# First row tile in chunks, second tile's gate values between the first one's up values, sigmoid table loaded later

## Chip, cores, metric

One core of a Trainium2 chip runs the kernel. The metric is the device time of one execution in microseconds; smaller is better. All runs told of here are at a granted clock of 0.999 or 1.0 in the records. Kernels are compared only within the same rounds. Times in the text are us. A time "at" which something happens counts from the start of the profiled span.

## The reference

```python
x = A_x                                   # 1 x 2048 x 640, bf16
xn = _layernorm(x, axis=-1)
s = _A_ref(xn, k_cache, v_cache, wq, wo)  # 32 heads of 192, the last 512 keys
g = _silu(_B_ref(xn, w_gate, w_up, w_down))
return x + s * g

def _B_ref(x, w_gate, w_up, w_down):      # 640 -> 1536 -> 640
    h = _sigmoid(x @ w_gate) * (x @ w_up)
    return h @ w_down
```

The kernel does the B part first, in four blocks of 512 rows. The first block is taken in four tiles of 128 rows, so that PE can begin as soon as 128 rows are normalised. The change touches nothing but these four tiles, and of those mostly the first two. The rest of the B part (until about 164 us in the trace) and the attention part behind it are the same in both kernels.

## The kernel before

```python
# loads: x of tile 0 on SP, x of tile 1 on ACT's queue, then the weights by pieces on SP
load_x(0, 1)
load_x(1, 1, nc.scalar)
load_f(nc.sync, wg_sb, wg_r, 0, 4, 0, 3)
load_f(nc.sync, wg_sb, wg_r, 0, 4, 3, NCD)
load_f(nc.sync, wu_sb, wu_r, 0, 4, 0, 3)      # "wu's first piece"
load_x(2, 1)
load_f(nc.sync, wu_sb, wu_r, 0, 4, 3, NCD)    # "wu's last chunks"
# ... cut ...

def stats_end(t):                             # rstd
    nc.vector.bn_aggr(mv[:], ln[t][:])
    if t == 0:
        nc.scalar.activation(rstd[:], mv[:, 1:2], AF.Sqrt, bias=eps_t[:], scale=1.0)
        nc.scalar.activation(junk[:], eps_t[:], AF.Sigmoid)   # loads the sigmoid table
        stats_half(1, 0)
        nc.vector.reciprocal(rstd[:], rstd[:])
    else:
        nc.vector.tensor_scalar(rstd[:], mv[:, 1:2], eps, None, op0=ALU.add)
        nc.gpsimd.tensor_tensor(rstd[:], rstd[:], mhalf[:], ALU.pow)

def turn_pe(t):          # 5 transposes on PE into PSUM, then two copies to xnT (3 + 2 chunks)
    engs = (nc.vector, nc.scalar) if t == 0 else (nc.scalar, nc.scalar)
    # ... cut ...

def tile_gates(t, amid): # 20 matmuls with wg, 20 with wu; turn_pe(t + 1) inside the wu ones
    for half, w in ((0, wg_sb), (1, wu_sb)):
        for c in range(NCD):
            if half == 1 and c == amid:
                turn_pe(t + 1)
            for f in range(FT):
                nc.tensor.matmul(bank[k][:, half, f * P:(f + 1) * P], ...)
    # sigmoid on ACT, product on VectorE: cut

dummy(18); dummy(6, 64)                       # idle matmuls that bring PE to full clock speed
# ... tile 0's statistics ...
normal(0, ((0, 3 * P), (3 * P, D)))
stats_half(1, 1)
turn_pe(0)
dummy(2)
# ... tiles 1 to 3 normalised ...
m0 = tile_gates(0, 3)                         # then tiles 1, 2, 3
# ... cut ...
for f in range(FT, NF):
    gated(0, f, k, norm_piece(1, f - FT))     # "the first gated block" begins here
```

The softmax here doesn't subtract the row's maximum and nothing guards it: scores larger than these inputs give would overflow.

Of the kernel before, what the change touches and what calls it, by code (L numbers as in the profile page):

```python
# [8 lines left out]
AF = mybir.ActivationFunctionType  # L9
ALU = mybir.AluOpType  # L10
BF16 = mybir.dt.bfloat16
# [4 lines left out]
def kernel(  # L16
# [13 lines left out]
    nc = tc.nc  # L30
    P = 128
    H2 = 64

    xf = A_x.flatten_outer_dims()
    of = out.flatten_outer_dims()
    S, D = xf.shape
# [8 lines left out]
    TB = 512  # L45
    NB = S // TB
    TQ = TB // P
    NT = S // P
    NCD = D // P
    NF = F // P  # L50
# [6 lines left out]
    eps = 1e-5  # L57
# [11 lines left out]
    bank = [psum.tile([P, 2, 512], F32, name=f"bank{i}") for i in range(4)]  # L69
# [4 lines left out]
    ident = const.tile([P, P], BF16, name="ident")  # L74
    mhalf = const.tile([P, 1], F32, name="mhalf")
    eps_t = const.tile([P, 1], F32, name="eps_t")
    junk = const.tile([P, 1], F32, name="junk")
    warm = const.tile([P, 256], BF16, name="warm")

    xnT = pers.tile([P, NB, NCD, TB], BF16, name="xnT")  # L80
# [5 lines left out]
    wg_r = B_w_gate.rearrange("(c p) f -> p c f", p=P)  # L86
# [56 lines left out]
    with ExitStack() as bctx:  # L143
        wB = bctx.enter_context(tc.tile_pool(name="wB", bufs=1))
        xpool = bctx.enter_context(tc.tile_pool(name="xpool", bufs=4))
        bwork = bctx.enter_context(tc.tile_pool(name="bwork", bufs=4))
        hpool = bctx.enter_context(tc.tile_pool(name="hpool", bufs=2))

        wg_sb = wB.tile([P, NCD, F], BF16, name="wg_sb")
        wu_sb = wB.tile([P, NCD, F], BF16, name="wu_sb")  # L150
# [1 line left out]

        xt = {}

        def load_x(t, n, eng=nc.sync):

            x = xpool.tile([P, n, D], BF16, name=f"x_sb{n}", bufs=4 if n == 1 else 2)
            if eng is nc.scalar:

                nc.vector.memset(x[:, 0, 0:2], 0.0)  # L160
            eng.dma_start(x[:], xf[t * P:(t + n) * P, :].rearrange("(q p) d -> p q d", p=P))  # L161
            for i in range(n):
                xt[t + i] = x[:, i, :]

        def load_f(eng, w, r, f0, f1, c0=0, c1=NCD):
            eng.dma_start(w[:, c0:c1, f0 * P:f1 * P], r[:, c0:c1, f0 * P:f1 * P])  # L166

        nc.vector.memset(warm[:], 0.0)
        load_x(0, 1)
        load_x(1, 1, nc.scalar)  # L170
        load_f(nc.sync, wg_sb, wg_r, 0, 4, 0, 3)
        load_f(nc.sync, wg_sb, wg_r, 0, 4, 3, NCD)
        load_f(nc.sync, wu_sb, wu_r, 0, 4, 0, 3)
        load_x(2, 1)
        load_f(nc.sync, wu_sb, wu_r, 0, 4, 3, NCD)
        load_x(3, 1)
# [3 lines left out]
        load_x(TQ, TQ)  # L180
        nc.sync.dma_start(wd_sb[:], wd_r)
        load_x(2 * TQ, TQ)
        nc.vector.memset(eps_t[:], eps)
        nc.scalar.activation(junk[:], eps_t[:], AF.Sqrt)
        nc.gpsimd.memset(mhalf[:], -0.5)
        make_identity(nc, ident[:])
# [2 lines left out]
        def dummy(n, cols=256):  # L189
            for _ in range(n):  # L190
                nc.tensor.matmul(bank[1][:, 1, 0:cols], lhsT=warm[:, 0:P], rhs=warm[:, 0:cols],
                                 start=True, stop=True)

        ln = {}

        def stats_half(t, i):
            if i == 0:
                ln[t] = bwork.tile([P, 2, nc.vector.BN_STATS_DIM], F32, name="st")
            nc.vector.bn_stats(ln[t][:, i, :], xt[t][:, i * (D // 2):(i + 1) * (D // 2)])

        def stats_end(t):
            mv = bwork.tile([P, nc.vector.BN_AGGR_DIM], F32, name="mv")
            rstd = bwork.tile([P, 1], F32, name="rstd")
            nc.vector.bn_aggr(mv[:], ln[t][:])
            if t == 0:
                nc.scalar.activation(rstd[:], mv[:, 1:2], AF.Sqrt, bias=eps_t[:], scale=1.0)
                nc.scalar.activation(junk[:], eps_t[:], AF.Sigmoid)
                stats_half(1, 0)
                nc.vector.reciprocal(rstd[:], rstd[:])
            else:  # L210
                nc.vector.tensor_scalar(rstd[:], mv[:, 1:2], eps, None, op0=ALU.add)
                nc.gpsimd.tensor_tensor(rstd[:], rstd[:], mhalf[:], ALU.pow)
            ln[t] = mv, rstd

        def normal(t, parts=((0, D),)):
            mv, rstd = ln[t]
            xn = xpool.tile([P, D], BF16, name="xn")
            for d0, d1 in parts:
                nc.vector.tensor_scalar(xn[:, d0:d1], xt[t][:, d0:d1], mv[:, 0:1], rstd[:, 0:1],
                                        op0=ALU.subtract, op1=ALU.mult)  # L220
            ln[t] = xn

        def turn_pe(t):

            engs = (nc.vector, nc.scalar) if t == 0 else (nc.scalar, nc.scalar)
            parts = []
            for i, (c0, c1) in enumerate(((0, 3), (3, NCD))):
                bk = bank[3][:, t % 2, :] if t or i == 0 else bank[2][:, 0, :]
                pT = bk[:, 0:NCD * H2].bitcast(BF16).rearrange("p (c n) -> p c n", c=NCD)
                for c in range(c0, c1):  # L230
                    nc.tensor.transpose(pT[:, c, :], ln[t][:, c * P:(c + 1) * P], ident[:])  # L231
                parts.append((engs[i], xnT[:, 0, c0:c1, t * P:(t + 1) * P], pT[:, c0:c1, :]))
            for eng, dst, src in parts:
                if eng is nc.vector:
                    nc.vector.tensor_copy(dst, src)
                else:
                    nc.scalar.activation(dst, src, AF.Copy)

        def turn_dma(t):
            q = t % TQ  # L240
# [2 lines left out]
        hT = {}  # L243
# [25 lines left out]
        def norm_piece(b, i):  # L269

            t = b * TQ + i

            def step():
                if i > 0:
                    normal(t - 1)
                    turn_dma(t - 1)
                if i < TQ:
                    stats_half(t, 0)
                    stats_half(t, 1)
                    stats_end(t)  # L280

            return step if i <= TQ else None


        FT = 4

        def tile_gates(t, amid):

            if 0 not in hT:
                hT[0] = hpool.tile([P, NF, TB], BF16, name="hT")  # L290
            k = t % 3
            r = slice(t * P, (t + 1) * P)



            for half, w in ((0, wg_sb), (1, wu_sb)):
                for c in range(NCD):
                    if half == 1 and c == amid:
                        turn_pe(t + 1)
                    for f in range(FT):  # L300
                        nc.tensor.matmul(bank[k][:, half, f * P:(f + 1) * P],  # L301
                                         lhsT=w[:, c, f * P:(f + 1) * P], rhs=xnT[:, 0, c, r],
                                         start=(c == 0 and f == 0), stop=(c == NCD - 1),
                                         skip_group_check=True)
            sig = bwork.tile([P, TB], BF16, name="sig")
            nc.scalar.activation(sig[:], bank[k][:, 0, :], AF.Sigmoid)
            return lambda: nc.vector.tensor_tensor(
                hT[0][:, 0:FT, r], bank[k][:, 1, :].rearrange("p (f n) -> p f n", f=FT),
                sig[:].rearrange("p (f n) -> p f n", f=FT), ALU.mult)

        dummy(18)
        dummy(6, 64)
        stats_half(0, 0)
        stats_half(0, 1)
        stats_end(0)
        normal(0, ((0, 3 * P), (3 * P, D)))
        stats_half(1, 1)
        turn_pe(0)
        dummy(2)
        stats_end(1)  # L320
        normal(1)
        stats_half(2, 0)
        stats_half(2, 1)
        stats_end(2)
# [1 line left out]
        stats_half(3, 1)  # L326
        normal(2)
        stats_end(3)
        m0 = tile_gates(0, 3)
        m0()  # L330
        normal(3)
        m1 = tile_gates(1, 1)
        m1()
        m2 = tile_gates(2, 1)
        m2()
        m3 = tile_gates(3, None)
        m3()
        k = 1
        for f in range(FT, NF):
            gated(0, f, k, norm_piece(1, f - FT))  # L340
            k = (k + 1) % 4
        for b in range(1, NB):
            for f in range(2):
                gated(b, f, k)
                k = (k + 1) % 4
            for q in range(TQ):
                down(b - 1, q, k)
                k = (k + 1) % 4
            if b == 1:
                load_x(3 * TQ, TQ)  # L350
            for f in range(2, NF):
                gated(b, f, k, norm_piece(b + 1, f - 4) if b + 1 < NB and f >= 4 else None)
                k = (k + 1) % 4
# [6 lines left out]
        for q in range(TQ):  # L360
            down(NB - 1, q, k)
            k = (k + 1) % 4
# [12 lines left out]
        for u in range(2):  # L375
            qT[u] = qpool.tile([P, 2 * DJ, TB], BF16, name="qT")
            for m in range(DJ):
                k = next(ks)
# [257 lines left out]
```

## Time and profile before

| | before |
|---|---|
| time, median of the runs (range) | 922.08 (921.9 to 922.63) |
| span of the profiled run | 920.8 |
| PE busy | 914.8, 99% |
| first matmul on wg | 6.20 |
| first gated block (L251) | 16.58 |
| from there to the end of the span | 904.2 |

### The profile page before, as it was taken

Reading aid. Unit: us, or ns where it says so; the run is one execution under the profiler, and the core shown is the slowest. Engines: PE = TensorE matmul, PEld = TensorE weight load, DVE = VectorE, ACT = ScalarE, POOL = GpSimd, SP = SyncE. Lnnn points to the kernel's source line nnn. Section 1 sums busy time; section 2 is a strip of 40 time slices with the busy share of each in tenths; the row PEclk is TensorE's granted clock in tenths of the full one; section 3 lists DMA queues with packets and bytes.
Section 4 is the critical chain, followed back from the end, with each engine's and each line's share of the span. In section 5 each row is a group of like instructions: output and inputs, shape, how many; then the busy total and the mean of one; then the engine's idle time right before and its main releaser. Section 6 shows DMA issues by size and latency. Waiting matters only on the chain.

```text
span 920.8 us, 25187 instructions
## 1 busy us (share of the span) xinstructions
PE 914.8 (99%) x11444; PEld 629.1 (68%) x11462; DVE 491.2 (53%) x982; ACT 302.3 (33%) x333; POOL 133.5 (15%) x158
## 2 busy tenths in 40 slices
PE   9999999999999999999999999999999999999998
PEld 7445455466868686767676777777776767686875
DVE  5452522445646464645555555545564646464677
ACT  4222222254142424233333333242414151515150
POOL 1000100001002000200120011001100111075633
PEclk9999999999999999999999999999999999999999
DMA  9320340115344434342426162616251615263535
GB/s 322 79 30 1 89 86 1 43 62 87 75 67 105 87 56 84 93 99 42 98 79 113 36 104 79 113 28 113 65 105 46 117 61 90 67 120 104 90 79 137
DMA packets 163147, 77.14 MB, mean 84 GB/s; under 512 B 140992, under 2 KB 158608, under 8 KB 163040
## 3 DMA queue, kind: packets, MB, share of 16 engines
q1 hardware_dynamic: 155936, 53.85, 29.9%
q0 software_dynamic: 5808, 20.52, 7.9%
q8 instruction: 89, 1.46, 0.7%
q10 hardware_dynamic: 1296, 1.16, 0.4%
q14 instruction: 18, 0.15, 0.1%
HBM read 39.45 MB, written 2.62 MB: 46 GB/s over the span
## 4 chain that ended last, share of the span: by engine, by line
PE 98%; DMA 1%; DVE 0%; SPq 0%; issue 0%; DVEq 0%
PE bank L494 22%; PE bank L423 21%; PE bank L445 19%; PE bank L405 18%; PE bank L251 10%; PE bank L263 6%; PE bank L371 1%; PE bank L301 1%; DMA wu_sb<-in_B_w_up_dram 1%; PE bank L529 0%; DVE o_sb L475 0%; DVE gate L480 0%; SPq L166 0%; SPq L161 0%; PE bank L231 0%
## 5 line engine op out<-in xcount | busy, mean ns | idle before, releaser
L409 ACT ACTIVATE E<-bank 128x1024 bf16<-128x1024 f32 x256 | 255.3, 1022 | 456.7 <-PE bank L405 456.6
L423 PE MATMUL bank<-xnT,wq_sb 64*128 64x512 bf16 x1800 | 226.4, 376 | 0.0
L494 PE MATMUL bank<-wo_sb,oT 64*128 64x320 bf16 x2688 | 205.2, 296 | 0.0
L405 PE MATMUL bank<-qT,kT 64*128 64x512 bf16 x1536 | 200.7, 376 | 0.0
L445 PE MATMUL bank<-vbuf,E 64*128 64x193 bf16 x4096 | 195.5, 243 | 0.0
L445 PEld LDWEIGHTS <-E 64*128 64x128 bf16 x4096 | 178.8, 94 | 10.4 <-issue 0.5
L494 PEld LDWEIGHTS <-oT 64*128 64x128 bf16 (+1 forms) x2892 | 163.3, 94 | 30.8 <-issue 0.5
L430 DVE CAST qT<-bank 128x1024 bf16<-128x1024 f32 x90 | 110.2, 1224 | 128.5 <-PE bank L423 128.5
L423 PEld LDWEIGHTS <-wq_sb 64*128 64x128 bf16 x1800 | 106.0, 100 | 87.1 <-issue 0.4
L405 PEld LDWEIGHTS <-kT 64*128 64x128 bf16 x1536 | 88.1, 94 | 73.5
L458 DVE TENSOR_TENSOR o_st<-bank,rden 128x768 bf16<-128x768 f32 x128 | 122.5, 957 | 4.8 <-DMA out_dram<-gate 0.4
L509 DVE TENSOR_TENSOR acc<-bank,acc 128x640 f32<-128x640 f32 x96 | 79.0, 823 | 20.3 <-PE bank L494 20.3
L118 POOL DMA_DIRECT2D vbuf<-in_A_v_cache_dram x28 | 21.1, 753 | 312.7 <-PE bank L445 309.8
L428 DVE COPY seen<-bank 128x2 f32<-128x2 f32 x90 | 14.3, 159 | 79.1 <-PE bank L423 79.1
L457 DVE RECIPROCAL rden<-bank 128x4 f32<-128x4 f32 x128 | 23.3, 182 | 60.6 <-PE bank L445 59.8
L251 PE MATMUL bank<-xnT,wg_sb 128*128 128x512 bf16 x216 | 54.5, 379 | 0.2
L251 PE MATMUL bank<-xnT,wu_sb 128*128 128x512 bf16 x215 | 54.4, 379 | 0.3
L257 DVE TENSOR_TENSOR hT<-bank,sig 128x512 bf16<-128x512 f32 x44 | 30.3, 689 | 42.7 <-ACT sig L254 42.7
L263 PE MATMUL bank<-wd_sb,hT 128*128 128x128 bf16 (+1 forms) x376 | 52.4, 297 | 0.4
L254 ACT ACTIVATE sig<-bank 128x512 bf16<-128x512 f32 x44 | 26.3, 597 | 68.4 <-PE bank L251 65.3
L263 PEld LDWEIGHTS <-hT 128*128 128x128 bf16 x384 | 29.7, 98 | 23.1
L251 PEld LDWEIGHTS <-wu_sb 128*128 128x128 bf16 x220 | 21.5, 98 | 26.0
(56 smaller groups left out, 366.6 us busy)
## 6 DMA issues: line engine op xcount, KB each, us to landing
wo_sb<-in_A_wo_dram SPq DMA_DIRECT2D x7, 960.0 KB, 5.5
wq_sb<-in_A_wq_dram POOLq DMA_DIRECT2D x7, 960.0 KB, 6.0
k_st<-in_A_k_cache_dram POOLq DMA_DIRECT2D x14, 384.0 KB, 5.4
vbuf<-in_A_v_cache_dram POOLq DMA_DIRECT2D x28, 192.0 KB, 3.6
row<-in_A_x_dram POOLq DMA_DIRECT2D x16, 160.0 KB, 2.8
oT<-o_st SPq DMA_TRANSPOSE x128, 3.4
x_sb<-in_A_x_dram SPq DMA_DIRECT2D x3, 640.0 KB, 9.9
wd_sb<-in_B_w_down_dram SPq DMA_DIRECT2D x1, 1920.0 KB, 13.5
```

Of the source, the lines that this page charges most:

```text
L251: nc.tensor.matmul(bank[k][:, half, 0:r1 - r0], lhsT=w[:, c, f * P:(f + 1) * P], rhs=xnT[:, b, c, r0:r1], start=(c == 0), stop=(c == NCD - 1))
L254: nc.scalar.activation(sig[:, 0:r1 - r0], bank[k][:, 0, 0:r1 - r0], AF.Sigmoid)
L257: nc.vector.tensor_tensor(hT[b][:, f, r0:r1], bank[k][:, 1, 0:r1 - r0], sig[:, 0:r1 - r0], ALU.mult)
L263: nc.tensor.matmul(wide(k)[:, d0:d1], lhsT=hT[b][:, f, q * P:(q + 1) * P], rhs=wd_sb[:, f, d0:d1], start=(f == 0), stop=(f == NF - 1))
L405: nc.tensor.matmul(bank[k][:, i, :], lhsT=kT[r, pr, j, c * P:(c + 1) * P], rhs=q[r, pr * DJ + j, :], start=(j == 0), stop=(j == DJ - 1))
L409: nc.scalar.activation(E[u, pr][:, c, :, :], bank[k][:], AF.Exp, scale=scale_qk)
L423: nc.tensor.matmul(bank[k][:, half, :], lhsT=wq[r, c, col:col + DJ * (P - 1) + 1:DJ], rhs=xnT[r, b, c, :], start=(c == 0 and not second), ...
L430: nc.vector.tensor_copy(qT[u][:, 2 * m:2 * m + 2, :], bank[k][:])
L445: nc.tensor.matmul(o4[:, q, 0:DH + 1], lhsT=e[r, c, h % 2, q * P:(q + 1) * P], rhs=vbuf[r, h, c, 0:DH + 1], start=(turn == 0 and qq == 0 a ...
L458: nc.vector.tensor_tensor(o_st[u][:, :, h * DH:(h + 1) * DH], o4[:, :, 0:DH], rden[:].to_broadcast([P, TQ, DH]), ALU.mult)
L494: nc.tensor.matmul(res[:, half, :], lhsT=oT[u][r, cc, q * P:(q + 1) * P], rhs=wo[r, cc, half * HD:(half + 1) * HD], start=(turn == 0 and c ...
L509: nc.vector.tensor_tensor(cols(acc[:, t, :]), res, cols(acc[:, t, :]), ALU.add)
```

## The change

Its intent is to give PE real work sooner. Tile 0 is normalised, turned and copied in pieces of one, two and two chunks of 128 columns, and each piece is multiplied when it is there, where before five chunks were turned together. Since all copies of tile 0 now go through ACT, the sigmoid table (1.28 of ACT time) is loaded only after the copies of tile 1. Tile 1's rstd uses ACT's square root, whose table is still loaded. Tile 1's 20 matmuls with wg go between tile 0's first and last matmuls with wu, so that wu's last chunks have longer to arrive. Wg's first piece moves to ACT's queue, tile 1's x to SP's.

```diff
-        load_x(1, 1, nc.scalar)
-        load_f(nc.sync, wg_sb, wg_r, 0, 4, 0, 3)
+        load_x(1, 1)
+        load_f(nc.scalar, wg_sb, wg_r, 0, 4, 0, 3)
 ... cut ...
-            if t == 0:
+            if t < 2:
                 nc.scalar.activation(rstd[:], mv[:, 1:2], AF.Sqrt, bias=eps_t[:], scale=1.0)
-                nc.scalar.activation(junk[:], eps_t[:], AF.Sigmoid)
-                stats_half(1, 0)
+                if t == 0:
+                    stats_half(1, 0)
                 nc.vector.reciprocal(rstd[:], rstd[:])
 ... cut: turn_pe(t, c0, c1, k) turns and copies a range of chunks, all copies on ACT;
     tile_gates becomes tile_half(t, half, c0, c1), tile_sigmoid(t), tile_gated(t) ...
-        normal(0, ((0, 3 * P), (3 * P, D)))
+        normal(0, ((0, P), (P, 3 * P), (3 * P, D)))
+
+        turn_pe(0, 0, 1)
+        turn_pe(0, 1, 3, 2)
+        tile_half(0, 0, 0, 1)
+        turn_pe(0, 3, NCD, 1)
+        tile_half(0, 0, 1)
         stats_half(1, 1)
-        turn_pe(0)
-        dummy(2)
         stats_end(1)
-        normal(1)
+        normal(1, ((0, 3 * P), (3 * P, D)))
+
+        tile_half(0, 1, 0, 2)
+        turn_pe(1, 0, 3)
+        tile_half(0, 1, 2, 3)
+        turn_pe(1, 3, NCD, 2)
+        nc.scalar.activation(junk[:], eps_t[:], AF.Sigmoid)
+        tile_half(1, 0)
+        tile_half(0, 1, 3)
+        tile_sigmoid(0)
 ... cut: tiles 2 and 3 as before, with turn_pe(t + 1) after the first chunk of wu ...
```

More of the change, by code (lines that the diff above doesn't have):

```diff
@@ L153, with load_x @@
         xt = {}
-        def load_x(t, n, eng=nc.sync):
+        def load_x(t, n):
             x = xpool.tile([P, n, D], BF16, name=f"x_sb{n}", bufs=4 if n == 1 else 2)
-            if eng is nc.scalar:
-                nc.vector.memset(x[:, 0, 0:2], 0.0)
-            eng.dma_start(x[:], xf[t * P:(t + n) * P, :].rearrange("(q p) d -> p q d", p=P))
+            nc.sync.dma_start(x[:], xf[t * P:(t + n) * P, :].rearrange("(q p) d -> p q d", p=P))
             for i in range(n):
@@ L168 @@
         nc.vector.memset(warm[:], 0.0)
+        nc.vector.memset(eps_t[:], eps)
+        nc.vector.memset(wg_sb[:, 0, 0:2 * P], 0.0)
         load_x(0, 1)
-        load_x(1, 1, nc.scalar)
-        load_f(nc.sync, wg_sb, wg_r, 0, 4, 0, 3)
+        load_x(1, 1)
+        load_f(nc.scalar, wg_sb, wg_r, 0, 4, 0, 3)
         load_f(nc.sync, wg_sb, wg_r, 0, 4, 3, NCD)
@@ L182 @@
         load_x(2 * TQ, TQ)
-        nc.vector.memset(eps_t[:], eps)
         nc.scalar.activation(junk[:], eps_t[:], AF.Sqrt)
@@ L221, in normal, with turn_pe @@
             ln[t] = xn
-        def turn_pe(t):
-            engs = (nc.vector, nc.scalar) if t == 0 else (nc.scalar, nc.scalar)
-            parts = []
-            for i, (c0, c1) in enumerate(((0, 3), (3, NCD))):
-                bk = bank[3][:, t % 2, :] if t or i == 0 else bank[2][:, 0, :]
-                pT = bk[:, 0:NCD * H2].bitcast(BF16).rearrange("p (c n) -> p c n", c=NCD)
-                for c in range(c0, c1):
-                    nc.tensor.transpose(pT[:, c, :], ln[t][:, c * P:(c + 1) * P], ident[:])
-                parts.append((engs[i], xnT[:, 0, c0:c1, t * P:(t + 1) * P], pT[:, c0:c1, :]))
-            for eng, dst, src in parts:
-                if eng is nc.vector:
-                    nc.vector.tensor_copy(dst, src)
-                else:
-                    nc.scalar.activation(dst, src, AF.Copy)
+        def turn_pe(t, c0=0, c1=NCD, k=3):
+            pT = bank[k][:, t % 2, 0:NCD * H2].bitcast(BF16).rearrange("p (c n) -> p c n", c=NCD)
+            for c in range(c0, c1):
+                nc.tensor.transpose(pT[:, c, :], ln[t][:, c * P:(c + 1) * P], ident[:])
+            for d0, d1 in ((c0, c1),) if c1 - c0 < NCD else ((0, 3), (3, NCD)):
+                nc.scalar.activation(xnT[:, 0, d0:d1, t * P:(t + 1) * P], pT[:, d0:d1, :], AF.Copy)
         def turn_dma(t):
@@ L285, with tile_half, tile_sigmoid, tile_gated @@
         FT = 4
-        def tile_gates(t, amid):
-            if 0 not in hT:
-                hT[0] = hpool.tile([P, NF, TB], BF16, name="hT")
-            k = t % 3
-            r = slice(t * P, (t + 1) * P)
-            for half, w in ((0, wg_sb), (1, wu_sb)):
-                for c in range(NCD):
-                    if half == 1 and c == amid:
-                        turn_pe(t + 1)
-                    for f in range(FT):
-                        nc.tensor.matmul(bank[k][:, half, f * P:(f + 1) * P],
-                                         lhsT=w[:, c, f * P:(f + 1) * P], rhs=xnT[:, 0, c, r],
-                                         start=(c == 0 and f == 0), stop=(c == NCD - 1),
-                                         skip_group_check=True)
-            sig = bwork.tile([P, TB], BF16, name="sig")
-            nc.scalar.activation(sig[:], bank[k][:, 0, :], AF.Sigmoid)
-            return lambda: nc.vector.tensor_tensor(
-                hT[0][:, 0:FT, r], bank[k][:, 1, :].rearrange("p (f n) -> p f n", f=FT),
-                sig[:].rearrange("p (f n) -> p f n", f=FT), ALU.mult)
+        hT[0] = hpool.tile([P, NF, TB], BF16, name="hT")
+        def tile_half(t, half, c0=0, c1=NCD):
+            w = (wg_sb, wu_sb)[half]
+            for c in range(c0, c1):
+                for f in range(FT):
+                    nc.tensor.matmul(bank[t % 3][:, half, f * P:(f + 1) * P],
+                                     lhsT=w[:, c, f * P:(f + 1) * P],
+                                     rhs=xnT[:, 0, c, t * P:(t + 1) * P],
+                                     start=(c == 0 and f == 0), stop=(c == NCD - 1),
+                                     skip_group_check=True)
+        sigs = {}
+        def tile_sigmoid(t):
+            sigs[t] = bwork.tile([P, TB], BF16, name="sig")
+            nc.scalar.activation(sigs[t][:], bank[t % 3][:, 0, :], AF.Sigmoid)
+        def tile_gated(t):
+            nc.vector.tensor_tensor(
+                hT[0][:, 0:FT, t * P:(t + 1) * P],
+                bank[t % 3][:, 1, :].rearrange("p (f n) -> p f n", f=FT),
+                sigs[t][:].rearrange("p (f n) -> p f n", f=FT), ALU.mult)
         dummy(18)
@@ L328 @@
         stats_end(3)
-        m0 = tile_gates(0, 3)
-        m0()
+        tile_gated(0)
         normal(3)
-        m1 = tile_gates(1, 1)
-        m1()
-        m2 = tile_gates(2, 1)
-        m2()
-        m3 = tile_gates(3, None)
-        m3()
+        for t in range(1, TQ):
+            if t > 1:
+                tile_half(t, 0)
+            tile_half(t, 1, 0, 1)
+            if t + 1 < TQ:
+                turn_pe(t + 1)
+            tile_half(t, 1, 1)
+            tile_sigmoid(t)
+            tile_gated(t)
         k = 1
```

## The prediction

> **What bounds the kernel now.** I read the page first: its head, the busy table and the chain that ended last.
>
> ```profile
> span 920.8 us, 25187 instructions
> PE 914.8 (99%) x11444; PEld 629.1 (68%) x11462; DVE 491.2 (53%) x982; ACT 302.3 (33%) x333; POOL 133.5 (15%) x158
> PE 98%; DMA 1%; DVE 0%; SPq 0%; issue 0%; DVEq 0%
> ```
>
> PE works all the way through and the chain lies 98% on it, so a microsecond saved or lost at the front moves the end by the same microsecond. But the change touches only what comes before the first `gated` block. So the question is a small one: how much PE idle time is there before that block (L251)? For this I read the timeline of the first 20 us and then the chain of waits of the first 40 us. Columns of the timeline: start, length, engine, line, operation, count.
>
> ```profile
> 4.60 1.28 ACT L207 ACT_TABLE_LOAD   x1
> 4.82 0.64 DVE L219 TENSOR_SCALAR xn<-x_sb,mv,rstd 128x384 bf16<-128x384 bf16 x2
> 5.25 0.71 PE L231 MATMUL bank<-ident,xn 128*128 128x128 bf16 x5
> 5.79 0.36 DVE L235 COPY xnT<-bank 128x384 bf16<-128x384 bf16 x1
> 6.01 0.38 ACT L237 ACTIVATE xnT<-bank 128x256 bf16<-128x256 bf16 x1
> 6.20 1.28 PE L301 MATMUL bank<-xnT,wg_sb 128*128 128x128 bf16 x20
> 7.62 0.67 PEld L301 LDWEIGHTS <-wu_sb 128*128 128x128 bf16 x12 [0.32 <-DMA wu_sb<-in_B_w_up_dram]
> 8.82 0.45 PEld L301 LDWEIGHTS <-wu_sb 128*128 128x128 bf16 x8 [0.25 <-DMA wu_sb<-in_B_w_up_dram]
> 9.33 1.28 PE L301 MATMUL bank<-xnT,wg_sb 128*128 128x128 bf16 x20
> 16.58 1.24 PE L251 MATMUL bank<-xnT,wg_sb 128*128 128x512 bf16 x4
> ```
>
> The first tile (normalise, turn, copy) reaches PE's first real matmul at 6.20. From there to 16.58, 10.38 us, PE has 160 matmuls and 15 transposes of 128 columns. From the start of 16 at 10.94 to the next group at 11.84 one takes 0.056 us, so 175 x 0.0555 = 9.71. The rest, 0.67, is the two waits for the up weights (gaps of 0.35 between 7.27 and 7.62, and 0.25 before 8.82) and some hundredths. From 9.33 on nothing is left to gain. The prize is therefore at most 0.6 us of waits, plus what the first matmul can come earlier.
>
> The chain from 3.37 to 8.83 is one transfer, not the normalisation:
>
> ```profile
> 3.37 5.41 DMA wu_sb<-in_B_w_up_dram
> 8.83 2.00 PE bank L301 x32
> ```
>
> In the trace's DMA records the first piece of wu was complete on fifteen of the sixteen DMA engines between 6.28 and 6.71 and on the sixteenth at 7.60. This one engine had a packet of 0.51 us at 4.52 (the median is 0.05), and it trails by 0.9 in every later transfer of that stretch. Without it, wu's pieces would be in at 6.7 and 7.9. I think that it is chance; the spread of the timed runs (921.9, 921.94, 922.63) is of the size of these waits.
>
> **What the Trainium skill says.** (1) "ScalarE: Activation LUTs", section "What ACT_TABLE_LOAD costs": 1.28 us for the load, 2.66 with a drain. The trace has the 1.28, but the next ACT instruction starts at 5.90, 0.02 after the load's end: no drain is seen. (2) "TensorE: Matmul & The Clock Gate", Part 1: the clock runs at half speed until a window of some 3.4 us has been busy, and the window's phase is free. The trace agrees by spacing though its clock row does not show it: the dummies of 256 columns start 0.213 us apart up to 5.1, the first transposes 0.107 apart, and from 6.2 on the matmuls 0.055. Full speed thus came between 5.8 and 6.2. (3) "DMA: Bandwidth & Descriptors", section "Issuing engines are not separate DMA queues": moving a load to another issuing engine saves only issue time. The stretch moves 350 GB/s whichever queue is used; x on ACT's queue did land in 2.4 us.
>
> **The change part by part.**
> - *Table load of sigmoid put later.* It ended at 5.88, its junk activation at 6.10, and the ACT copy began at 6.01. The fifth transpose's result was there at about 5.96, so the load held that copy back by 0.05. And PE was released at 6.20 by the DVE copy (5.79 to 6.15), not by ACT. Worth 0 to 0.05. In the new place it runs from about 9.2 to 10.5 on ACT, before the first sigmoid (about 10.6). It delays the copies of tile 2 to about 11.8, against a need at 11.9 (16 matmuls after 11.0): hidden, barely.
> - *First tile in chunks.* Rsqrt and the first chunk still start at 4.82. A 384-column part takes 0.378, a 256-column part 0.340, so 128 columns about 0.30: the first chunk is ready at 5.12 instead of 5.20. But the dummies hold PE until about 5.2, so the first transpose starts at 5.22, not 5.25. Its result takes 0.31 at the slow clock, and the ACT copy of 128 columns about 0.27 (the 384 and 256 forms: 0.490 and 0.379): first matmul at about 5.87 instead of 6.20, **0.33 earlier**.
> - *But PE then waits for the other chunks.* Chunks 1 and 2: xn at 5.40, transposes 5.44 and 5.55, ACT copy 5.90 to 6.28, matmuls from 6.33. Chunks 3 and 4 are turned only after the four matmuls of chunk 0 (from about 6.2), copied 6.5 to 6.9, multiplied from 6.95. The tile's gate values end at 7.4 to 7.5; before, 6.20 + 20 x 0.0555 = 7.31. All copies being on ACT one after the other, the lead is lost, with **0.1 to 0.15** on top.
> - *Weights on ACT's queue, x of tile 1 on SP's.* Bytes ahead of wu's first piece are the same 1.3 MB or so, hence the same landing, 6.7 or 7.6. x1 lands at about 3.5 to 4.0, needed at 4.17. Worth 0.
> - *Rstd of tile 1 by ACT and reciprocal.* Instead of an add (0.15), a POOL power (0.57) and gaps, sqrt (0.29) and reciprocal (0.16); but the sqrt sits behind the tile-0 copies on ACT and ends at about 7.1. Normalised tile 1 from about 7.75 instead of 7.59. PE comes to it only at 7.9 or 8.1. Worth 0.
> - *Tile 1's gate values between tile 0's up values.* Before: 12 up, 5 transposes, 8 up, 20 gate. After: 8 up, 3 transposes, 4 up, 2 transposes, 20 gate, 8 up. From the third transpose's start to the first gate matmul there is 0.22 + 0.04 + 0.49 (ACT copy) + 0.05 = 0.80, filled by only 0.39 of PE work (the transpose itself, four matmuls, two transposes): **a new wait of about 0.4**. It replaces the wait for wu's last chunks, which come before they are needed either way.
>
> The sum up to the end of tile 0 and of tile 1's gate, with the slow DMA engine: 7.62 + 10 x 0.0555 + 0.80 + 28 x 0.0555 = 10.53, against 10.44 before: **+0.1**. Without it: 7.45 + 2.91 = 10.36. Before it would be 7.31 + 0.67 (12 up) + 1.02 (five transposes and copy, partly filled by the 8 up) + 1.11 = 10.11: **+0.25**. The work after that is the same in both. So I expect between +0.1 and +0.25 us, some 0.02% of the time.
>
> **The rivals.**
> - *It gains 0.3 to 0.6 us* (921.4). For it: the earlier first matmul, and the 0.6 of waits for wu, which the new order was visibly made to fill; if the slow DMA engine is the rule and not chance, or the up weights come later in unprofiled runs, tile 1's gate work in front of wu's last chunks pays. Against it: tile 1's transposes are placed behind wu's first piece, so the first wait stays and only the second, 0.25, can be filled.
> - *It loses 1 to 2 us* (923.3). At the front PE is idle in patches (about 0.35 between 5.2 and 6.3) in the very window that brings full speed. If the change of clock slips by a window, some 60 matmuls take 0.107 instead of 0.056. Against it: five sixths of that window are still dummies. Another way to the same loss is an extra table load, if a copy was not to be had in the sqrt set, 1.28 each.
> - *ACT becomes the bound of this stretch:* late table load, sigmoid and copies of tile 2 in one queue. The margin is 0.1 us by my count; if it fails, PE waits some tenths before tile 2's gate values (922.4).
>
> **Range and chances.** The middle is 921.94 + 0.1, with a lean to the first rival because the order was chosen with some purpose: 922.0. The runs themselves spread by 0.7 us, the rivals reach from -0.6 to +2. 921.2 to 922.9 should hold it 8 times in 10. Two per cent is 18.4 us, more than the whole stretch of 16.58 that is touched, so within 2% is all but sure.
>
> **What would show it.** Right: the first matmul on wg at about 5.9 but tile 0's gate matmuls in three bursts, ended no earlier than 7.3; a wait of PE for wu again if its landing is at 7.6; a wait of some 0.4 before tile 1's gate values, put down to ACT's copy; the sigmoid's table load after 9; L251 starting between 16.5 and 16.9. Wrong: L251 at 16.2 or earlier (the wait was filled after all), or at 17.5 or later, with matmuls of 0.107 beyond 6.3 (the clock came late) or a third table load. If the time moves by more than 1 us while L251 starts where it did, the cause lies outside all of this.

## The result

| | before | changed |
|---|---|---|
| time, median (range), 4 runs each | 922.08 (921.9 to 922.63) | 922.48 (922.1 to 923.0) |
| span of the profiled run | 920.8 | 920.3 |
| first matmul on wg | 6.20 | 5.84 |
| first gated block | 16.58 | 16.31 |
| from there to the end | 904.2 | 904.0 |

The ratio is 1.0004, with a 95% interval from 0.9986 to 1.0021: the same, within 2%. A ratio here is the mean time of one kernel's runs over that of the other's of the same rounds, so it is not quite the ratio of the medians that are quoted. In the two other calls in which the changed kernel ran it was 1.0003 and 1.0001. All three lie above 1 and none is clear of it.

The timeline of the changed kernel's first 20 us (start, length, engine, line, operation, count, and in brackets the idle time before it and what ended it):

```profile
5.25 0.54 PE L226 MATMUL bank<-ident,xn 128*128 128x128 bf16 x3
5.51 0.69 ACT L228 ACTIVATE xnT<-bank 128x128 bf16<-128x128 bf16 x2 [0.87 <-PE bank L226]
5.84 0.38 PE L287 MATMUL bank<-xnT,wg_sb 128*128 128x128 bf16 x4
6.26 1.16 PE L287 MATMUL bank<-xnT,wg_sb 128*128 128x128 bf16 x16
7.25 0.61 PE L287 MATMUL bank<-xnT,wu_sb 128*128 128x128 bf16 x8
8.07 0.76 ACT L228 ACTIVATE xnT<-bank 128x384 bf16<-128x384 bf16 x2 [1.13 <-PE bank L226]
8.09 0.28 PE L226 MATMUL bank<-ident,xn 128*128 128x128 bf16 x2
8.61 1.28 PE L287 MATMUL bank<-xnT,wg_sb 128*128 128x128 bf16 x20 [0.24 <-ACT xnT L228]
8.85 1.28 ACT L326 ACT_TABLE_LOAD   x1
11.56 1.28 PE L287 MATMUL bank<-xnT,wg_sb 128*128 128x128 bf16 x20
16.31 1.24 PE L242 MATMUL bank<-xnT,wg_sb 128*128 128x512 bf16 x5
```

The first matmul comes 0.36 earlier, at 5.84. Tile 0's matmuls with wg are done at 7.25 instead of 7.31 (the last one starts at 7.20 and at 7.26): of the 0.36 less than 0.1 is left by then. At 8.61 there is a new wait. The last transpose was issued at about 8.15 and the next matmul starts at 8.61: some 0.4 in which PE waits for ACT's copy of tile 1's first three chunks (the page puts 0.24 of it down to ACT, since it counts the pipelined end of the transposes as busy). The chain of waits of the changed kernel, in order of time, says the same. Where the chain of before ran through the transfer of wu from 3.37 to 8.78, this one runs through ACT's copy:

```profile
8.07 0.50 ACT xnT L228
8.61 1.95 PE bank L287 x32
```

The sigmoid's table load lies at 8.85, and tile 2's gate values start at 11.56, right behind the 16 matmuls before them: the load is hidden.

That the first gated block starts 0.27 earlier in this pair of traces, while the timed runs are 0.4 slower in the median, is the question that the experiments have to answer. One trace of each kernel may not be a fair pair: in before's trace one DMA engine was 0.9 behind.

### The profile page after: what moved, and what is told of

Its sections match the earlier page's. It is cut to its first block, busy times and chain, and to the rows that moved or that the text cites. A ratio compares the mean times of both kernels' runs of the same rounds, so it can differ in the third digit from the quotient of the medians.

```text
span 920.3 us, 25202 instructions
## 1 busy us (share of the span) xinstructions
PE 915.1 (99%) x11460; PEld 628.5 (68%) x11460; DVE 491.7 (53%) x983; ACT 303.4 (33%) x336; POOL 133.6 (15%) x157
## 4 chain that ended last, share of the span: by engine, by line
PE 99%; DVE 0%; ACT 0%; DVEq 0%; issue 0%
PE bank L504 22%; PE bank L433 21%; PE bank L455 19%; PE bank L415 18%; PE bank L242 10%; PE bank L254 6%; PE bank L381 1%; PE bank L287 1%; PE bank L190 0%; PE bank L539 0%; DVE o_sb L485 0%; DVE gate L490 0%; PE bank L226 0%; ACT xnT L228 0%; DVEq L641 0%
## 5 line engine op out<-in xcount | busy, mean ns | idle before, releaser
L254 PE MATMUL bank<-wd_sb,hT 128*128 128x512 bf16 (+1 forms) x384 | 52.8, 299 | 0.0
```

The lines of the kernel that those rows point to most:

```text
L254: nc.tensor.matmul(wide(k)[:, d0:d1], lhsT=hT[b][:, f, q * P:(q + 1) * P], rhs=wd_sb[:, f, d0:d1], start=(f == 0), stop=(f == NF - 1))
```

## The experiments

My theory: at the front the change wins some tenths by the chunks and loses some by the new wait; what differs between two traces is mostly chance there (a lagging DMA engine, the moment at which PE comes to full clock speed); and from the first gated block on, time is passed to the end one for one. Rivals: the lag belongs to before's order of loads, and the new order is what cures it; or the front hardly matters to the end.

### c1 and c2: both kernels again

No edit.

> The kernel before, unchanged, as a control. Theory A (one DMA engine fell 0.9 us behind by chance in the profiled run of before): this trace shows the first piece of wu landed on all sixteen engines by about 6.7, no wait of PE for wu, and the first gated block between 16.0 and 16.3, which is earlier than the 16.31 of the changed kernel. Rival B (the lag comes with this kernel's order of loads): again a wait for wu at about 7.6 and the first gated block at 16.5 to 16.6. Either way the time against itself is 1.000, and the width of its interval tells what size of difference can be seen here at all.

> The changed kernel, unchanged. Both theories: first matmul on wg at 5.8 to 5.9, a wait of 0.4 before tile 1's gate values, first gated block between 16.2 and 16.6. Theory A: a lag of one DMA engine can turn up here as well. Time against before: between 0.9995 and 1.0008, not to be told from 1.

Before again: 922.58, ratio to itself 1.0 (0.9987 to 1.0012). The interval is 0.12% wide to either side, 1.1 us, so nothing of the size at stake can be seen in the times. Changed again: 922.6, 1.0003 (0.999 to 1.0015). PE's timeline of before again, and its weight loads in a second view:

```profile
6.20 1.28 PE L301 MATMUL bank<-xnT,wg_sb 128*128 128x128 bf16 x20 [0.15 <-DVE xnT L235]
7.38 0.84 PE L301 MATMUL bank<-xnT,wu_sb 128*128 128x128 bf16 x12
16.33 1.03 PE L251 MATMUL bank<-xnT,wg_sb 128*128 128x512 bf16 x3
```

```profile
8.55 0.45 PEld L301 LDWEIGHTS <-wu_sb 128*128 128x128 bf16 x8 [0.23 <-DMA wu_sb<-in_B_w_up_dram]
```

PE's timeline of the changed kernel again:

```profile
5.87 0.59 PE L287 MATMUL bank<-xnT,wg_sb 128*128 128x128 bf16 x4
7.73 0.62 PE L287 MATMUL bank<-xnT,wu_sb 128*128 128x128 bf16 x8
9.10 1.28 PE L287 MATMUL bank<-xnT,wg_sb 128*128 128x128 bf16 x20 [0.24 <-ACT xnT L228]
16.80 0.38 PE L242 MATMUL bank<-xnT,wg_sb 128*128 128x512 bf16 x1
```

The pair has changed places: before 16.33, changed 16.80. The DMA records say why. In before's second trace wu's first piece was complete on the last engine at 7.35 and not at 7.60. In the changed kernel's second trace one engine came at 7.70, when the other fifteen had come by 7.01. The landings of all fourteen traces agree: 7.5 or later in one of the four with before's order of queues (before) and in three of the ten with the new one (7.70 in c2, 7.66 in d1, 7.62 in e1). The big lag is not tied to either order; rival B falls. What makes it is not shown, and it was smaller in c1, not gone: the last three engines came at 7.1 to 7.35, the others by 6.8. My expectation that before would show no wait for wu at all was wrong, though: wu's last chunks came at 8.53 (7.9 was the estimate), and PE waited for them. Two ranges were missed as well: c1's first gated block came at 16.33, not at 16.0 to 16.3 and not before the changed kernel's 16.31, and c2's at 16.80, not at 16.2 to 16.6. The second source of spread is PE's clock. In the changed kernel's second trace the four matmuls from 5.87 on start 0.107 apart, so full speed came at 6.36. In its first trace it was there by 5.0: the last idle matmuls, of 64 columns, start 0.03 apart from there on and 0.053 where the clock is slow. In c2 the late clock is hidden: the matmuls with wg end at 7.50, and PE waits for wu until 7.73 anyway.

### c3: tile 0's last up values first

```diff
-        tile_half(1, 0)
         tile_half(0, 1, 3)
+        tile_half(1, 0)
```

> The changed kernel with one part undone: tile 0's last up values (8 matmuls) before tile 1's gate values, as before. My theory (the new order opens a wait of 0.4 while tile 1's first chunks are copied, and wu's last chunks are there in time): the wait before tile 1's gate values shrinks from 0.4 to 0.1 or less and the first gated block starts about 0.3 earlier than in the changed kernel, near 16.0. Rival (the order is right, since wu's last chunks come late): PE waits for wu instead, until 8.3 to 8.8, and the first gated block starts no earlier than 16.3. The time alone moves by 0.03%, too little to be seen.

PE's timeline:

```profile
8.43 0.62 PE L287 MATMUL bank<-xnT,wu_sb 128*128 128x128 bf16 x8
8.89 1.28 PE L287 MATMUL bank<-xnT,wg_sb 128*128 128x128 bf16 x20
16.23 1.03 PE L242 MATMUL bank<-xnT,wg_sb 128*128 128x512 bf16 x3
```

The time is 922.29, 0.9997 (0.9985 to 1.001). The wait before tile 1's gate values is gone: they follow the 8 up matmuls without a gap. But these 8 themselves wait until 8.43, because wu's last chunks land at 8.41. So the first gated block starts at 16.23 and not at 16.0: of the 0.3 expected, 0.1 is seen. My theory is right that the new order opened a wait, and wrong that the old order had none; each order has one, of 0.4 for ACT's copy in the one and 0.2 for the weights in the other.

### c4: sigmoid's table early

```diff
-            if t < 2:
+            if t == 0:
                 nc.scalar.activation(rstd[:], mv[:, 1:2], AF.Sqrt, bias=eps_t[:], scale=1.0)
-                if t == 0:
-                    stats_half(1, 0)
+                nc.scalar.activation(junk[:], eps_t[:], AF.Sigmoid)
+                stats_half(1, 0)
 ...
-        nc.scalar.activation(junk[:], eps_t[:], AF.Sigmoid)
         tile_half(1, 0)
```

> The changed kernel with the table of sigmoid loaded where it was, right behind the first square root; the rstd of tile 1 has to go back to the add and the power with it. My theory: alone the later load is worth 0.05, but with all copies of tile 0 on ACT it is what makes the chunks possible: here ACT is in the load until 5.9, the copy of the first chunk starts at about 6.0 instead of 5.5, the first matmul at about 6.3 instead of 5.84, and the first gated block 0.1 to 0.4 later than in the changed kernel. Rival (the load costs nothing in either place): first matmul at 5.8 to 5.9.

The timeline, ACT's part and PE's:

```profile
4.58 1.28 ACT L206 ACT_TABLE_LOAD   x1
5.98 0.53 ACT L228 ACTIVATE xnT<-bank 128x128 bf16<-128x128 bf16 x2
```

```profile
6.29 0.38 PE L287 MATMUL bank<-xnT,wg_sb 128*128 128x128 bf16 x4 [0.59 <-ACT xnT L228]
16.76 0.38 PE L242 MATMUL bank<-xnT,wg_sb 128*128 128x512 bf16 x1
```

Time 922.72, 1.0003 (0.9989 to 1.0016). PE waits for ACT until 6.29, 0.45 later than in the changed kernel, and the first gated block starts 0.45 later too. The weights were there (wu's first piece by 7.20, needed at 7.70). Tile 1's rstd went back to the old way too, but that is not the cause: its transposes start at 8.15, right behind the 8 up matmuls. With the chunks, the later table load is worth the whole lead that the chunks give.

### d3: the later table load alone, in the kernel before

```diff
-                nc.scalar.activation(junk[:], eps_t[:], AF.Sigmoid)
                 stats_half(1, 0)
 ...
         turn_pe(0)
+        nc.scalar.activation(junk[:], eps_t[:], AF.Sigmoid)
         dummy(2)
```

> The kernel before with one part of the change alone: the table of sigmoid is loaded after tile 0's copies. My theory: PE was released by the DVE copy and not by ACT, so the first matmul stays at 6.15 to 6.25 and the first gated block between 16.3 and 16.6; the ACT copy starts at 5.9 to 6.0 instead of 6.01. Rival (the load was the hindrance): first matmul at 5.9.

```profile
6.26 1.62 PE L300 MATMUL bank<-xnT,wg_sb 128*128 128x128 bf16 x20
16.67 1.24 PE L250 MATMUL bank<-xnT,wg_sb 128*128 128x512 bf16 x4
```

Time 922.31, 0.9999 (0.9985 to 1.0013). In PE's timeline the first matmul is at 6.26: alone the later load brings nothing, since PE is released by VectorE's copy. The ACT copy started at 6.06, no earlier than 6.01 before. The 20 matmuls take 1.62 instead of 1.28 because full speed came only at 6.99 in this trace; these 0.34 are enough to put the first gated block (16.67) a little past the expected range.

### d2: no warm-up matmuls

```diff
-        dummy(18)
-        dummy(6, 64)
```

> The changed kernel without the 24 idle matmuls at the start. It measures what the slow clock costs and how close the changed order is to losing it. My theory (full speed comes only after a busy window, whatever the matmuls are for): the matmuls from 5.8 to about 9 or 10 start 0.107 apart instead of 0.056, some 60 of them, and the first gated block starts 1 to 2.5 us later, at 17.5 to 19. Rival (the clock does not depend on the warm-up here): first gated block at 16.3 to 16.8.

```profile
6.78 1.91 PE L287 MATMUL bank<-xnT,wg_sb 128*128 128x128 bf16 x16
18.14 1.03 PE L242 MATMUL bank<-xnT,wg_sb 128*128 128x512 bf16 x3
```

Time 924.36, 1.0018 (1.0002 to 1.0033). The matmuls start 0.107 apart up to 9.98 and 0.055 apart from 10.05 on, about 4.5 after PE's first instruction at 5.53. The first gated block is 1.8 later than in the changed kernel, and the time grows by about as much. The warm-up is needed, and by this measure a late clock is the largest risk of the front, larger than anything that the change moves.

### e2: the queues as before

```diff
-        load_x(1, 1)
-        load_f(nc.scalar, wg_sb, wg_r, 0, 4, 0, 3)
+        load_x(1, 1, nc.scalar)
+        load_f(nc.sync, wg_sb, wg_r, 0, 4, 0, 3)
 ... cut: load_x takes a queue again, and the memset that goes with a load on ACT's queue moves from wg to x ...
```

> The changed kernel with one part undone: the first piece of wg on SP's queue and tile 1's x on ACT's, as before. My theory (the bytes ahead of wu's first piece are the same, so the queue does not matter): x1 lands at 3.5 instead of 4.0, wg's first piece within 0.2 of 4.9 to 5.1, wu's first piece at 7.1 to 7.6 but for a lagging engine, first gated block at 16.3 to 16.8 as with the changed kernel. Rival (the second queue brings the weights earlier): wu's first piece later by 0.3 or more than in the changed kernel.

Time 922.47, 1.0 (0.9986 to 1.0014). First matmul 5.79, first gated block 16.25. Landings of the last engine: x of tile 1 at 3.54 (changed kernel 4.00), wg's first piece at 5.08 (5.10), wu's first piece at 6.96 (7.09, 7.70 and 7.28 in the changed kernel's three traces). The second queue brings the weights no earlier. Wu's landing and the first gated block even lie just before the expected 7.1 and 16.3.

### d1 and e1: how much of the front reaches the end

```diff
             tile_gated(t)
+        dummy(20)          # e1: dummy(40)
         k = 1
```

> The changed kernel with 20 idle matmuls of 256 columns ahead of the first gated block, 20 x 0.107 = 2.1 us of PE work that nothing needs. My theory (PE is the bound from there to the end, so a microsecond at the front is a microsecond at the end): the first gated block starts at 18.4 to 18.9, the span grows by 2.1 against the changed kernel and the time is about 924.6, 1.002 of before. Rival (later waits swallow the front): the time grows by less than 1 us.

> The changed kernel with 40 idle matmuls ahead of the first gated block, 40 x 0.107 = 4.3 us. With 20 of them the span grew by 3.3 against another run of the changed kernel, not by 2.1; in its trace 0.45 was lost in a pause of PE's issue at 209.7 and 0.7 in a longer wait of PE for a VectorE product near 885. Theory A (the front counts one for one, and the surplus is a wait that depends on how other engines' work falls, not on the length of the delay): the span grows by 4.3 plus 0 to 1.0. Rival B (a microsecond at the front costs one and a half at the end): the span grows by 6 to 7.

With 20 idle matmuls (2.1) the time is 925.73, 1.0035 (1.0021 to 1.0049), which is 3.2 over before; with 40 (4.3) it is 927.3, 1.0052 (1.0039 to 1.0066), 4.8 over before. The second pair of 2.1 costs 1.6 and the first 3.2. The intervals are 1.3 to either side, so the times alone say little: d1's holds the expected 924.6 and rival B's one and a half for one. Rival B falls by e1: its interval ends at 6.1, and its span is 5.0 longer than e3's and not 6 to 7.

The traces settle more than the times. VectorE's 128 reciprocals of the attention, from about 202 on, stand in every trace, and each can be compared with the same one of e3. The distance at the first of them is the distance at the front (-0.19 in e4, +0.43 in c2, +1.77 in d2, +4.71 in e1), and in eleven of the thirteen other traces it stays the same, to 0.01, up to 868. So a microsecond at the front stays one for 850 us. The two exceptions step once, near 210: before from +0.21 to +0.35, d1 from +2.56 to +3.16. Behind that, between 874 and 890, every trace but c1 loses something against e3: 0.06 to 0.8.

In d1 both losses can be found. PE stands still for 0.42 up to 210.36 with "issue" as the reason, which I can't explain (its weight loads stand still for 0.65). And near 885 there are these lines, of VectorE's, POOL's and PE's timelines:

```profile
883.48 2.25 DVE L491 TENSOR_TENSOR gate<-o_sb,acc 128x640 bf16<-128x640 f32 x1
```

```profile
883.62 1.41 POOL L524 TENSOR_TENSOR acc<-acc,gate 128x640 f32<-128x640 f32 x1
```

```profile
886.51 0.84 PE L456 MATMUL bank<-vbuf,E 64*128 64x193 bf16 x16 [0.57 <-DVE o_sb L486]
```

VectorE's sum takes 0.82 when alone. Here it takes 2.25, which is 0.82 + 1.41 and 0.02 more: it stood still for as long as POOL's product. The next product on VectorE, which frees the bank that PE is waiting for, is that much later; PE waits 0.57, and the whole step is 0.8. The Trainium skill has this ("SBUF — State Buffer", section "Who interferes with whom": a VectorE instruction with two SBUF inputs contends with a GpSimd instruction that reads SBUF, and issue order decides which one is blocked). That the two contend, the trace shows. Which one is blocked, it doesn't settle: by the profile VectorE began first here, by 0.14, and was the one that stood still. Where POOL began first (e4 below), VectorE was held too, as the page has it. All the sums that were held, this one too, end 0.68 to 0.69 after POOL's instruction.

### d4, e3, e4: an attempt at a better version, twice, and the changed kernel once more

```diff
         turn_pe(0, 1, 3, 2)
-        tile_half(0, 0, 0, 1)
         turn_pe(0, 3, NCD, 1)
+        tile_half(0, 0, 0, 1)
 ...
-        tile_half(1, 0)
         tile_half(0, 1, 3)
+        tile_half(1, 0)
```

> An attempt at a better version: the changed kernel with tile 0's last up values before tile 1's gate values, and with chunks 3 and 4 of tile 0 turned before the first four matmuls instead of behind them. My theory: their copy then starts at about 6.2 instead of 6.4, the gate values of tile 0 run without a wait, and the first gated block starts at 16.0 to 16.2 where no DMA engine lags. Rival (the slow clock and the wait for wu at 7.2 take it back): 16.2 to 16.4, as with the order alone. The time: 0.9995 to 1.000 of before, not to be told from 1.

> The changed kernel once more, beside the better version on the same chip. Theory (what differs between runs of one kernel at the front is when full clock speed comes and whether a DMA engine lags): first gated block 16.3 if full speed is there by 5.5 and wu's first piece has landed by 7.3, up to 16.8 otherwise. Time against before between 0.9995 and 1.0008.

> The better version of d4 once more, to see whether its small lead (0.9996) holds up. Theory (worth 0.3 to 0.5 us over the changed kernel at the front): first gated block at 16.0 to 16.35, time 0.9993 to 0.9999 of before and below that of the changed kernel in the same call. Rival (chance): time at or above 1.000.

| | time | ratio to before | first gated block | span |
|---|---|---|---|---|
| d4, better version | 922.09 | 0.9996 (0.9984 to 1.0009) | 16.33 | 920.6 |
| e4, the same | 922.28 | 0.9998 (0.9984 to 1.0012) | 16.18 | 920.4 |
| e3, changed kernel | 922.55 | 1.0001 (0.9988 to 1.0014) | 16.37 | 920.3 |

Twice slightly below before and 0.27 below the changed kernel: in the expected direction, but not told apart from chance by any interval. D4's 16.33 lies in the rival's range, e4's 16.18 in that of the theory. D4's front was late because wu's first piece came at 7.40 and its last chunks at 8.59; e4 had full speed only at 6.63.

The spans hold a surprise. E4 starts the first gated block 0.19 before e3 and yet ends no earlier (920.4 against 920.3). VectorE's, POOL's and PE's timelines of e4 near 880, and then VectorE's and PE's of e3:

```profile
873.35 0.82 DVE L485 TENSOR_TENSOR o_sb<-bank,gate 128x640 f32<-128x640 f32 x1 [1.30 <-PE bank L504]
880.13 1.72 DVE L490 TENSOR_TENSOR gate<-o_sb,acc 128x640 bf16<-128x640 f32 x1
```

```profile
879.77 1.40 POOL L524 TENSOR_TENSOR acc<-acc,row 128x640 f32<-128x640 f32 x1 [1.46 <-DMA row<-in_A_x_dram]
```

```profile
882.63 0.84 PE L455 MATMUL bank<-vbuf,E 64*128 64x193 bf16 x16
```

```profile
873.54 0.82 DVE L485 TENSOR_TENSOR o_sb<-bank,gate 128x640 f32<-128x640 f32 x1 [1.30 <-PE bank L504]
880.32 0.84 DVE L490 TENSOR_TENSOR gate<-o_sb,acc 128x640 bf16<-128x640 f32 x1
```

```profile
882.60 0.85 PE L455 MATMUL bank<-vbuf,E 64*128 64x193 bf16 x16
```

At 873.35 the lead of 0.19 is still whole. Then VectorE's sum meets a sum of POOL (879.77 to 881.17 in e4) and takes 1.72 instead of 0.84. PE's 16 matmuls, which wait for the product behind it, start at 882.63 in the one and at 882.60 in the other. The lead of the front is given back there. The same sum takes 1.63 in c3 and 1.81 in e2, which also start early (16.23, 16.25), but also 1.79 in d4 and 1.89 in d3, and only 0.82 to 0.84 in both traces of before, in all three of the changed kernel and in c4. So it depends on where POOL's instructions happen to fall, and not on the front alone. Other sums of this kind are held elsewhere, also in these last traces: in c2 the one at 877.27 takes 1.64, and c2's distance to e3 grows from 0.43 to 0.68 right behind it.

## Why the prediction was right, point by point

- **Size and place.** Forecast were 922.0 in 921.2 to 922.9, all but sure within 2%; measured was 922.48. That the time fell inside says little, since the range is 1.7 wide, and part of it is luck: the fronts of the traces explain no more than 0.2 of the 0.4 between the medians. The lean from +0.1 down to 922.0, for a purpose behind the new order, was not borne out: the three ratios 1.0004, 1.0003 and 1.0001 are +0.1 to +0.4 us, where the sum of the steps had +0.1 to +0.25. No interval settles the sign. The prediction's own mark, L251 between 16.5 and 16.9, was met by one trace of the changed kernel in three (16.80); 16.31 and 16.37 lie between this mark and the one for wrong, 16.2.
- **Table load.** Right in both places: worth nothing alone (d3), hidden at 8.85, and what c4 adds: with the chunks it is worth 0.45.
- **First matmul.** Forecast 5.87, seen 5.84 to 5.87 in the changed kernel's three traces.
- **Then PE waits for the other chunks.** The mechanism was right (three bursts; a lead of 0.36 falls to less than 0.1), the size was 0.2 off where full speed came early: the gate matmuls ended at 7.25 and not at 7.4 to 7.5, since I took the clock of before's one trace (about 6.0) as given. Where it came at 6.36 (c2) they ended at 7.50. One reading was a slip: before's first wait for wu runs from 7.31 to 7.62, 0.3 and not 0.35; nothing rests on it.
- **Queues.** Right: wu's first piece lands no earlier with the change (e2).
- **The new wait of 0.4.** Right: about 0.4 before tile 1's gate values (at 8.61, 8.67 and 9.10) in all three traces of the changed kernel. The sentence beside it, that wu's last chunks come before they are needed either way, was wrong: they land at 8.2 to 8.5 even without the big lag, and undoing the order swaps 0.4 for 0.2 (c3).
- **The balance of the front.** Forecast with the slow DMA engine was +0.1, without it +0.25. The traces give 16.80 against 16.58 with it (+0.2), and 16.31 and 16.37 against 16.33 without it (0). Both small, as said. The second term was mis-sized by the two points above: by the end of this work (tile 0's up values and tile 1's gate values) the forecast had 10.36 against 10.11, and the traces have 10.16 against 10.19 in c1. But the clocks of these pairs differ too (5.0 against about 4.7, 6.36 against about 6.2), so they are no clean comparison.
- **The slow engine is chance.** Right: it turned up again in the changed kernel (c2) and was smaller in before (c1); three of ten traces with the new order have it and one of four with the old one.
- **A microsecond at the front is one at the end.** Right up to 868, to 0.01 but for one step near 210 in two traces, and only about right to the end. It was read from the chain that lies 98% on PE. The contention of VectorE and POOL between 874 and 890, some 860 us behind the change, then takes a few tenths that differ from trace to trace: e4's lead of 0.19 over e3 never arrived.
- **The rivals.** A gain of 0.3 to 0.6 was not there in the traces (the intervals of the times would allow it), a late clock did not come with the change (full speed came at 5.0, 6.36 and 5.0 in its three traces, and at about 6.2 and 4.7 in before's two), and ACT did not become the bound.

Open is how much of the +0.1 to +0.4 in the timed runs is real, what stopped PE's issue before 210.36 in d1 and, for less, near 210 in before, and why a DMA engine now and then falls behind.

## What to carry to other kernels

Before cutting a front shorter, add up how much idle time PE has there (here waits of some 0.6 in 920) and compare it with the spread of the runs (0.7 here): below that, only traces can judge, and more than one of each kernel. A piece that arrives sooner helps only until PE meets the next piece, so write down the arrival of every chunk and not of the first alone. And a lead at the front is not in hand until the end: a wait elsewhere that depends on how two other engines' instructions fall can give it back.

## What the Trainium skill lacked or had wrong

- "TensorE: Matmul & The Clock Gate", Part 1, puts the change to full speed at around 4 us of sustained work, give or take half a microsecond. With the same warm-up, from 1.06 on, it came between 4.2 (d1) and 6.99 (d3) here, 3.1 to 5.9 later. In d3 the late change is worth 0.34: 20 matmuls take 1.62 instead of 1.28.
- The same page warns that recorded clock events have been unreliable, but no page says that the profile's clock row can read full speed all through, as here (9 tenths or more in every slice of all fourteen traces), while the matmuls start 0.107 apart for 128 columns; the spacing has to be read.
- "ScalarE: Activation LUTs", section "What ACT_TABLE_LOAD costs", adds a drain of 1.38 to the load. Here the next ACT instruction starts 0.01 to 0.02 after the load's 1.28.
- "DMA: Bandwidth & Descriptors", section "Latency and other measured facts", names two engines that are usually slower and puts this down, as a guess, to the GpSimd path alone. Here, on the sync engine's queue, one engine of sixteen (which one was not read) fell behind by 0.9 (before, with a packet of 0.51 where the median is 0.05) and by 0.7 (c2), and every later landing of that stretch carried it.
- No page names a pause of PE's issue such as the 0.42 before 210.36 in d1, which cost 0.60.
- "SBUF — State Buffer", section "Who interferes with whom", gives no size. Here every sum of VectorE that was held by POOL, some 40 in fourteen traces, ended 0.68 to 0.69 after POOL's instruction, where it takes 0.82 to 0.84 alone.
